# Splitting a product's result straight out of PSUM on ACT and DVE, and one ACT function for product and sigmoid

## The chip, the cores and the metric

The kernel runs on one core of one Trainium2 chip. The engines are PE (matmul), DVE (vector), ACT (scalar functions), POOL (general) and SP (issues DMAs). The metric is the device time of one execution in microseconds (us); the time of a kernel is the median of its runs.

## What is computed

Inputs are f32 or wider; NT = 2304 tokens of width 512. Attention with a pooled and a local part comes first, then a mixture of experts with one expert a token, then a dense two-layer block:

```
x = attention(q, k, v)                              # 2304 x 512
xc = x[x @ w_skip > 0];  e_idx = argmax(xc @ w_gate)
for e in range(8):                                  # w1[e] 512 x 1024, w2[e] 1024 x 512
    h = np.maximum(xc[mask] @ w1[e], 0.0)
    y[mask] = gate_w[mask, None] * (h @ w2[e])
out[do_compute] = xc + y
h = x @ w_in                                        # 512 x 2048
g = h * (1.0 / (1.0 + np.exp(-1.702 * h)))
return g @ w_out                                    # 2048 x 512
```

## The kernel before

Each large product is done in f16 with split operands: a value v becomes a high part (v scaled by a power of two, rounded to f16) and a low part (the scaled value minus the high part, again f16). A product is then three: high x high, high x low, low x high, added in PSUM. So each operand is split on the way, and the name of a tile tells its part: xh and xl, wh and wl, hh and hl, gh and gl.

The program has three stages, `phase_a` (attention and routing, and the split of w_in), `phase_b` (the experts) and `phase_c` (the last block); `overflow` between the last two is a loop that runs only where an expert has more than 192 tokens.

In `phase_b` every expert takes 192 token rows. The steps of an expert are small functions, and a table, `STAGE_B`, gives each a due time in periods of an expert. All steps of all experts are sorted by (expert + due time) and emitted in that order; `in_order` then ties each of PE, ACT, DVE and POOL to this order. So every engine is a queue in a written order, in which steps of three neighbouring experts are mixed. The steps that matter here:

- `load`: SP loads the f32 weights, raw, in four parts of 1 MB; a part's buffer is free again when its wl is made.
- `bound`, `scale`, `scb`: ACT squares and sums the raw weights (jk, L689), PE sums over partitions (psw, L59), DVE makes the scale by some tiny operations (w_e, w_s, w_i, L72 to L78), then iv (L706, L708), the factor that takes the scales back.
- `hi`, `lo`: wh on ACT for one half of a matrix (L715) and on DVE for the other (L717); wl on DVE (L723).
- `gather`, `xprep`, `xh`, `xl`: POOL gathers the token rows by indirect DMA (L768), PE transposes them, ACT and DVE split them.
- `l1`, four parts of two 128-wide columns of the hidden layer: 24 matmuls (L812) into one PSUM tile ph, from a pool of four that also serves psw.
- `l1e`: ACT takes Relu of ph with the factor 2^-20 to an f32 tile ht (L820; two buffers). `l1h`: DVE casts ht to hh (L823). `l1l`: POOL subtracts, hl = ht - hh (L827).
- `l2`, four parts (L839, L846): the second product, from hh, hl and the split w2.
- `giv`, `yrow`, `ymx`, `yadd`, `scatter`: ACT scales the rows of y (L865), DVE takes their maximum (L871), POOL adds them to the token rows (g, L881) and scatters these by indirect DMA (L902). `scat` on POOL writes token numbers (ids, L911).

In one period the written order on DVE is, with the expert in brackets: xl(0), lo00(0), lo10(-1), l1h2(-1), ymx(-2), l1h3(-1), hi11(-1), hi01(0), lo11(-1), lo01(0), l1h1(0), l1h0(0), scb(0), giv(-1). On ACT: l1e2(-1), bound00(1), l1e3(-1), three bounds, l1e0(0), l1e1(0), xh(1), hi00(1), hi10(0), yrow(-1). On PE: xprep(1), l10(0), l11(0), l20 to l22(-1), scale(0), l23(-1), l12(0), l13(0). On POOL: l1l1(-1), scat0(0), l1l2(-1), gather(2), l1l3(-1), yadd0(-2), scatter0(-2), scat2(-1), yadd1(-2), scatter1(-2), scat1(0), l1l0(0).

In `phase_c` the tokens go in six blocks of 384. `l1` of a block has 16 steps of 12 matmuls (L1097) into ph, a PSUM tile from a pool of three; ACT takes the sigmoid with a scale (L1101), DVE multiplies with ph and a factor (sg, L1102), and one step later `late` casts sg to gh on ACT (L1089) and subtracts to gl (L1090), on POOL in the first three blocks and on DVE after that. `l2` of a block (L1117) follows two blocks behind. During the first two and a half blocks `Wout` splits w_out: on ACT w64a (L126), w64j (L231) and woh (L242), on DVE w64l and w64f (L130 to L132) and wol (L243); these steps are put behind the steps of `l1` by `behind`, which holds them to the order in which they are emitted.

Of the kernel before, what the change touches and what calls it, by code (L numbers as in the profile page):

```python
# [18 lines left out]
P = 128  # L19
# [15 lines left out]
CAP = 192  # L35
# [3 lines left out]
XW = 2 * XH  # L39
NB = 384  # L40
NTC = NB // P
C20 = 2.0 ** -20
ONE = float(1 << 23)

# [22 lines left out]
    return ps[:, P:P + 1]  # L67


def pow2_into(nc, e, s, si, m, squared):  # L70
    V = nc.vector
    V.tensor_scalar(e, m.bitcast(I32), 0x7F800000, None, op0=ALU.bitwise_and)  # L72
    if squared:
        V.tensor_scalar(e, e, 0.5, 64.0 * ONE, op0=ALU.mult, op1=ALU.add)
        V.tensor_scalar(e, e, 0x7F800000, None, op0=ALU.bitwise_and)
    V.tensor_scalar(e, e, 64.0 * ONE, 200.0 * ONE, op0=ALU.max, op1=ALU.min)
    V.tensor_scalar(s.bitcast(I32), e, -1.0, 268.0 * ONE, op0=ALU.mult, op1=ALU.add)  # L77
    V.tensor_scalar(si.bitcast(I32), e, 14.0 * ONE, None, op0=ALU.subtract)  # L78


def pow2_scale(nc, pool, m, name, squared=False):


    e = pool.tile([P, 1], I32, name=f"{name}_e")
    s = pool.tile([P, 1], F32, name=f"{name}_s")
    si = pool.tile([P, 1], F32, name=f"{name}_i")
    pow2_into(nc, e, s, si, m, squared)
    return s, si


# [7 lines left out]
    csc=3.1751, chl=5.4280)  # L98

STAGE_B = dict(  # L100
    l10=-2.8750, l1e0=-2.5414, l1h0=-2.1815, l1l0=-2.0258, l20=-1.6661, l11=-2.8473, l1e1=-2.5379, l1h1=-2.2714,
    l1l1=-1.8902, l21=-1.5453, l12=-2.1639, l1e2=-1.9897, l1h2=-1.8716, l1l2=-1.8041, l22=-1.3442, l13=-2.0520,
    l1e3=-1.8744, l1h3=-1.8562, l1l3=-1.7262, l23=-1.2374, scale=-2.2810, scb=-2.1764, bound00=-3.9127,
    hi00=-3.1600, lo00=-2.9149, load00=-2.9138, bound01=-3.5859, hi01=-2.6890, lo01=-2.5881, load01=-2.5870,
    bound10=-2.7781, hi10=-2.1111, lo10=-1.8915, load10=-1.8904, bound11=-2.5563,
    hi11=-1.7296, lo11=-1.6624, load11=-1.6613, gather=-4.7500, xprep=-3.9203, xh=-3.5055, xl=-2.9872,
    giv=-1.1000, yrow0=-1.0047, yrow1=-1.0040, ymx=-0.8644, yadd0=-0.6966, scatter0=-0.6711,
    yadd1=-0.6113, scatter1=-0.6009, scat0=-2.8208, scat1=-2.5500, scat2=-1.6433)


# [554 lines left out]
class Experts:  # L665
# [30 lines left out]
    def scale2(self, i, ix):  # L696
        nc, sm = self.nc, self.sm
        m2 = self.m2.pop(i)
        e = sm.tile([P, 2], I32, tag="w_e", name="w_e")
        s, si = (sm.tile([P, 2], F32, tag=f"w_{n}", name=f"w_{n}", bufs=3) for n in ("s", "i"))  # L700
        pow2_into(nc, e, s, si, m2, True)
        for wi in range(2):
            self.s[i + 1 - wi, wi] = s[:, wi:wi + 1], si[:, wi:wi + 1]
        if i >= 0:
            iv = sm.tile([P, 1], F32, tag="iv", name="iv")
            nc.vector.scalar_tensor_tensor(iv, self.s[i, 0][1], 1.0 / C20, self.s[i, 1][1],  # L706
                                           op0=ALU.mult, op1=ALU.mult)
            nc.vector.tensor_tensor(iv, iv, ix, ALU.mult)  # L708
            self.iv[i] = iv

    def hi(self, e, wi, hf, on_act):
# [15 lines left out]
def phase_b(ctx, tc, c, ex):  # L727
    nc = tc.nc
    ident = c["ident"]
    V, A, G, T = nc.vector, nc.scalar, nc.gpsimd, nc.tensor  # L730
    wk = ctx.enter_context(tc.tile_pool(name="b_wk", bufs=2))
    sm = ctx.enter_context(tc.tile_pool(name="b_sm", bufs=2))
# [23 lines left out]
    V.tensor_reduce(xb, c["xm"], axis=AX.X, op=ALU.max)  # L756
    mp = max_all(nc, c, psh.tile([P, 512], F32, tag="psh", name="psm"), sm.tile([1, 1], F32, name="xb0", bufs=1), xb)
    V.tensor_copy(c["xmax"], mp)
    sx, ix = pow2_scale(nc, c["cp"], c["xmax"], "sx")
    ex.onesf, ex.ps = c["onesf"], lambda: psh.tile([P, 512], F32, tag="psh", name="psw")  # L760

    xg, xs, hts, gv, phs, pxs, pys, hr, yr = {}, {}, {}, {}, {}, {}, {}, {}, {}

    def gather(e):
        g0 = wk.tile([P, XW], F32, tag="g0", name="g0", bufs=5)
# [48 lines left out]
                    n += 1  # L814
        phs[e, fp] = ph

    def l1e(e, fp):
        ph, (hh, hl) = phs.pop((e, fp)), hts[e]
        hr[e, fp] = t = wk.tile([P, 2, CAP], F32, tag="ht", name="ht")
        A.activation(t, ph, AF.Relu, scale=C20)  # L820

    def l1h(e, fp):
        V.tensor_copy(hts[e][0][:, 2 * fp:2 * fp + 2, :], hr[e, fp])  # L823

    def l1l(e, fp):
        hh, hl = hts[e]
        G.tensor_tensor(hl[:, 2 * fp:2 * fp + 2, :], hr.pop((e, fp)), hh[:, 2 * fp:2 * fp + 2, :], ALU.subtract)  # L827

    def l2(e, i):

# [195 lines left out]
def phase_c(ctx, tc, c, win, wih, wil, w_out, out):  # L1026
    nc = tc.nc
    ident = c["ident"]
    V, A, T = nc.vector, nc.scalar, nc.tensor
# [27 lines left out]
    sinv = sm.tile([P, 1], F32, name="sinv")
    V.tensor_reduce(sinv, win.si, axis=AX.X, op=ALU.max)
# [73 lines left out]
    n, m = steps[-1][0] + 2, ahead * (DF // P) + DF // P // 2  # L1132
# [146 lines left out]
```

## Time and profile before

| | us |
|---|---|
| median of 3 runs | 803.38 (798.86 to 803.81) |
| the profiled execution | 801.5, its span 799.7 |
| busy PE / DVE / ACT / POOL | 694.6 / 478.1 / 394.0 / 297.7 |
| mean granted clock of PE | 0.948 of full speed |

The span is the time from the first to the last instruction that the profiler saw; what lies around it is 1.8 us. Busy time is a mean over stages that differ, so a stage is read by itself: the experts run from about 205 to 387 us, the last stage from about 393 us to the end.

### The profile page before, as it was taken

How to read it: one execution, taken by the hardware profiler on the slowest of the kernel's cores; microseconds unless marked ns; L12 is line 12 of the kernel's file. 1: busy time of each engine (PE TensorE's matmuls, PEld its weight loads, DVE VectorE, ACT ScalarE, POOL GpSimd, SP SyncE). 2: the span in 40 equal slices, each digit the busy share in tenths (PEclk: the TensorE clock that was granted, in tenths of full speed). 3: DMA queues.
4: the chain of work that ended last, by engine and by line, in shares of the span. 5: the costliest groups of instructions: out<-in, count | busy, mean ns of one | idle time of the engine just before them, and what ended most of it. 6: DMA issues, size and time to landing. Idle time of an engine off the chain costs nothing.

```text
span 799.7 us, 15485 instructions
## 1 busy us (share of the span) xinstructions
PE 694.6 (87%) x6207; PEld 430.8 (54%) x6207; DVE 478.1 (60%) x909; ACT 394.0 (49%) x806; POOL 297.7 (37%) x294
## 2 busy tenths in 40 slices
PE   4478978878499899878499899999999999999997
PEld 3355655655376666655265555545545545544443
DVE  8889997996588888899468996204503511520000
ACT  1566665763687667763167876414413412421111
POOL 8555644650346999987334444300000000000000
PEclk9977997999599999999799999999999999999999
DMA  9956998617456666520344331001000000000000
GB/s 259 263 152 174 301 285 260 158 33 258 113 205 237 241 234 240 189 73 16 119 132 146 123 102 27 1 26 54 1 27 14 1 13 27 1 14 27 27 27 27
DMA packets 43007, 92.49 MB, mean 116 GB/s; under 512 B 10398, under 2 KB 24354, under 8 KB 38837
## 3 DMA queue, kind: packets, MB, share of 16 engines
q1 hardware_dynamic: 25908, 81.11, 31.6%
q10 hardware_dynamic: 14208, 4.87, 2.6%
q0 software_dynamic: 2816, 5.50, 2.4%
q8 instruction: 50, 0.82, 0.4%
q14 instruction: 25, 0.20, 0.1%
HBM read 79.55 MB, written 12.92 MB: 116 GB/s over the span
## 4 chain that ended last, share of the span: by engine, by line
PE 48%; DVE 19%; POOL 11%; issue 9%; DMA 8%; ACT 4%; SPq 1%; POOLq 0%; ACTq 0%; DVEq 0%
PE po L1117 22%; PE ph L1097 17%; DMA w64r<-in_moe_w_in 5%; POOL hl L827 3%; DVE wl L723 3%; POOL g L881 3%; DVE w64l L131 2%; POOL ids L911 2%; POOL g L768 2%; DVE sg L1102 2%; DVE w64f L132 1%; DVE wol L243 1%; PE po L464 1%; DVE w64l L130 1%; DMA vw<-in_vwin 1%
## 5 line engine op out<-in xcount | busy, mean ns | idle before, releaser
L1102 DVE SCALAR_TENSOR_TENSOR sg<-ph,gs,sg 128x384 f32<-128x384 f32 x96 | 58.7, 615 | 132.3 <-ACT sg L1101 132.1
L1097 PEld LDWEIGHTS <-wih 128*128 128x128 f16 x768 | 76.2, 100 | 60.1 <-issue 12.4
L1123 ACT ACTIVATE o<-po,os 128x128 f32<-128x128 f32 x72 | 20.5, 367 | 148.8 <-PE po L1117 93.4
L1117 PEld LDWEIGHTS <-gh 128*128 128x128 f16 x576 | 56.3, 98 | 66.0
L1097 PE MATMUL ph<-xh,wih 128*128 128x384 f16 x384 | 79.5, 330 | 8.4 <-DVE sg L1102 7.5
L723 DVE SCALAR_TENSOR_TENSOR wl<-raw,w_s,wh 128x2048 f16<-128x2048 f32 x32 | 81.3, 2574 | 4.4 <-ACT wh L715 2.9
L1097 PE MATMUL ph<-xh,wil 128*128 128x384 f16 x384 | 79.9, 330 | 0.0
L1090 POOL TENSOR_TENSOR gl<-sg,gh 128x384 f16<-128x384 f32 x48 | 49.2, 1027 | 81.7 <-ACT gh L1089 63.2
L1097 PE MATMUL ph<-xl,wih 128*128 128x384 f16 x384 | 78.9, 328 | 0.0
L1089 ACT CAST gh<-sg 128x384 f16<-128x384 f32 x96 | 48.8, 509 | 47.8 <-DVE sg L1102 47.6
L1101 ACT ACTIVATE sg<-ph,ih 128x384 f32<-128x384 f32 x96 | 55.4, 578 | 33.2 <-PE ph L1097 31.1
L1117 PE MATMUL po<-woh,gh 128*128 128x512 f16 x288 | 67.1, 379 | 0.0
L689 ACT ACTIVATE jk<-raw 128x2048 f16<-128x2048 f32 x32 | 61.1, 1908 | 9.3 <-DVE mx L686 8.7
L1117 PE MATMUL po<-wol,gh 128*128 128x512 f16 x288 | 65.3, 379 | 0.0
L1117 PE MATMUL po<-woh,gl 128*128 128x512 f16 x288 | 65.1, 379 | 0.0
L827 POOL TENSOR_TENSOR hl<-ht,hh 128x384 f16<-128x384 f32 x32 | 43.5, 1372 | 27.2 <-DVE hh L823 17.4
L1097 PEld LDWEIGHTS <-wil 128*128 128x128 f16 x384 | 38.0, 99 | 25.5 <-issue 1.2
L812 PEld LDWEIGHTS <-wh 128*128 128x128 f16 x512 | 44.1, 101 | 4.4 <-ACT wh L715 2.3
L1117 PEld LDWEIGHTS <-gl 128*128 128x128 f16 x288 | 28.2, 98 | 34.0
L715 ACT ACTIVATE wh<-raw,w_s 128x2048 f16<-128x2048 f32 x16 | 31.3, 1995 | 29.6 <-DVE w_s L77 18.2
L1090 DVE TENSOR_TENSOR gl<-sg,gh 128x384 f16<-128x384 f32 x48 | 26.8, 558 | 26.5 <-ACT gh L1089 26.5
L812 PE MATMUL ph<-xh,wl 128*128 128x192 f16 x256 | 32.7, 252 | 3.9 <-DVE wl L723 3.6
(228 smaller groups left out, 1343.5 us busy)
## 6 DMA issues: line engine op xcount, KB each, us to landing
raw<-in_moe_w SPq DMA_DIRECT2D x32, 1024.0 KB
w64r<-in_moe_w_in SPq DMA_DIRECT2D x16, 512.0 KB
w64r<-in_moe_w_out SPq DMA_DIRECT2D x16, 512.0 KB
vw<-in_vwin SPq DMA_DIRECT2D x32, 216.0 KB
qt<-in_q SPq DMA_DIRECT2D x16, 288.0 KB
kt<-in_k SPq DMA_DIRECT2D x16, 288.0 KB
vn<-in_v SPq DMA_DIRECT2D x16, 288.0 KB
xd<-xn ACTq DMA_DIRECT2D x16, 288.0 KB
```

The costliest lines, as they stand in the source:

```text
L689: self.nc.scalar.activation(j, r, AF.Square, accum_out=self.mx[i][:, hf, wi:wi + 1])
L715: self.nc.scalar.activation(t, r, AF.Copy, scale=s)
L723: self.nc.vector.scalar_tensor_tensor(t, r, s, self.h[e, wi, hf], op0=ALU.mult, op1=ALU.subtract)
L812: T.matmul(ph[:, fi, :], wa[:, k_, o:o + P], xa[:, k_, :], start=(n == 0), stop=(n == 3 * NK - 1))
L827: G.tensor_tensor(hl[:, 2 * fp:2 * fp + 2, :], hr.pop((e, fp)), hh[:, 2 * fp:2 * fp + 2, :], ALU.subtract)
L881: G.tensor_tensor(g, g, yr[e][:, cols(ti)].rearrange("p (h w) -> p h w", w=DM // 2), ALU.add)
L1089: A.copy(split[1], split[0])
L1090: (nc.gpsimd if b <= ahead else V).tensor_tensor(split[2], split[0], split[1], ALU.subtract)
L1097: T.matmul(ph, wa[:, k_, f * P:(f + 1) * P], xx[:, k_, :], start=(n == 0), stop=(n == 3 * NK - 1))
L1101: A.activation(sg, ph, AF.Sigmoid, scale=ih[:, f:f + 1])
L1102: V.scalar_tensor_tensor(sg, ph, gs[:, f:f + 1], sg, op0=ALU.mult, op1=ALU.mult)
L1117: T.matmul(po, ga[:, f, i * P:(i + 1) * P], wa[:, f, :], start=(n == 0), stop=(n == 3 * (DF // P) - 1))
```

## The change

In the experts `l1e` and ht go. ACT writes hh from ph directly, as f16 (`l1h`), at the due times that `l1e` had; DVE makes hl from ph and hh (`l1l`), at the due times that `l1h` had; POOL has no part in it any more. The powers of two move: the scales s get other constants (t, XT, WT), so that ph needs no factor, and iv is one operation and no longer two. In the last stage ACT has one function, Gelu_apprx_sigmoid of the scaled ph, which is the product of its argument with the sigmoid of 1.702 times it; `late` then makes gh on ACT with a scale and gl on DVE in all blocks, from sg and gh.

```
+XT, WT = 3, 8
-def pow2_into(nc, e, s, si, m, squared):
+def pow2_into(nc, e, s, si, m, squared, t=15):
...
-    V.tensor_scalar(s.bitcast(I32), e, -1.0, 268.0 * ONE, op0=ALU.mult, op1=ALU.add)
-    V.tensor_scalar(si.bitcast(I32), e, 14.0 * ONE, None, op0=ALU.subtract)
+    V.tensor_scalar(s.bitcast(I32), e, -1.0, (253.0 + t) * ONE, op0=ALU.mult, op1=ALU.add)
+    V.tensor_scalar(si.bitcast(I32), e, (t - 1.0) * ONE, None, op0=ALU.subtract)
...
-    l10=-2.8750, l1e0=-2.5414, l1h0=-2.1815, l1l0=-2.0258, ...
+    l10=-2.8750, l1h0=-2.5414, l1l0=-2.1815, ...
...
-            nc.vector.scalar_tensor_tensor(iv, self.s[i, 0][1], 1.0 / C20, self.s[i, 1][1],
-                                           op0=ALU.mult, op1=ALU.mult)
-            nc.vector.tensor_tensor(iv, iv, ix, ALU.mult)
+            nc.vector.scalar_tensor_tensor(iv, self.s[i, 0][1], ix, self.s[i, 1][1], op0=ALU.mult, op1=ALU.mult)
...
-    def l1e(e, fp):
-        ph, (hh, hl) = phs.pop((e, fp)), hts[e]
-        hr[e, fp] = t = wk.tile([P, 2, CAP], F32, tag="ht", name="ht")
-        A.activation(t, ph, AF.Relu, scale=C20)
-
     def l1h(e, fp):
-        V.tensor_copy(hts[e][0][:, 2 * fp:2 * fp + 2, :], hr[e, fp])
+        A.activation(hts[e][0][:, 2 * fp:2 * fp + 2, :], phs[e, fp], AF.Relu)

     def l1l(e, fp):
-        hh, hl = hts[e]
-        G.tensor_tensor(hl[:, 2 * fp:2 * fp + 2, :], hr.pop((e, fp)), hh[:, 2 * fp:2 * fp + 2, :], ALU.subtract)
+        hh, hl = (h[:, 2 * fp:2 * fp + 2, :] for h in hts[e])
+        V.scalar_tensor_tensor(hl, phs.pop((e, fp)), 0.0, hh, op0=ALU.max, op1=ALU.subtract)
...
-    V.tensor_scalar(ih, win.si, ix, 1.702, op0=ALU.mult, op1=ALU.mult)
-    gs = sm.tile([P, NF], F32, name="gs")
-    V.tensor_scalar(gs, win.si, smin, C20, op0=ALU.mult, op1=ALU.mult)
+    V.tensor_scalar(ih, win.si, ix, None, op0=ALU.mult)
+    gs = sm.tile([P, 1], F32, name="gs")
+    V.tensor_scalar(gs, sx, smin, C20, op0=ALU.mult, op1=ALU.mult)
...
-                A.copy(split[1], split[0])
-                (nc.gpsimd if b <= ahead else V).tensor_tensor(split[2], split[0], split[1], ALU.subtract)
+                A.activation(split[1], split[0], AF.Copy, scale=gs)
+                V.scalar_tensor_tensor(split[2], split[0], gs, split[1], op0=ALU.mult, op1=ALU.subtract)
...
-            A.activation(sg, ph, AF.Sigmoid, scale=ih[:, f:f + 1])
-            V.scalar_tensor_tensor(sg, ph, gs[:, f:f + 1], sg, op0=ALU.mult, op1=ALU.mult)
+            A.activation(sg, ph, AF.Gelu_apprx_sigmoid, scale=ih[:, f:f + 1])
```

## Rows read from the trace of the kernel before

**Rows 1.** Windows, one expert: length; busy us PE, PEld, DVE, ACT, POOL; clock; DMA; GB/s.

```profile
299.91:320.82 20.91, 18.22 (x180) 13.21 (x180) 18.50 (x23) 15.03 (x18) 19.04 (x13) 1.00 0.67 240
```

**Rows 2.** Timeline, DVE, experts: start, us, engine, line, operation, idle before and releaser.

```profile
223.88 0.15 DVE L72 TENSOR_SCALAR w_e<-psw 128x2 int32<-128x2 int32 x1
...
298.97 5.27 DVE L723 SCALAR_TENSOR_TENSOR wl<-raw,w_s,wh 128x2048 f16<-128x2048 f32 x2
304.16 1.69 DVE L823 CAST hh<-ht 128x384 f16<-128x384 f32 x2
305.77 0.15 DVE L72 TENSOR_SCALAR w_e<-psw 128x2 int32<-128x2 int32 x1
...
309.00 4.62 DVE L723 SCALAR_TENSOR_TENSOR wl<-raw,w_s,wh 128x2048 f16<-128x2048 f32 x2
314.95 0.53 DVE L823 CAST hh<-ht 128x384 f16<-128x384 f32 x1 [1.33 <-ACT ht L820]
...
317.21 0.36 DVE L823 CAST hh<-ht 128x384 f16<-128x384 f32 x1 [0.88 <-ACT ht L820]
317.49 2.48 DVE L717 TENSOR_SCALAR wh<-raw,w_s 128x2048 f16<-128x2048 f32 x2
319.88 2.35 DVE L723 SCALAR_TENSOR_TENSOR wl<-raw,w_s,wh 128x2048 f16<-128x2048 f32 x1
...
367.91 0.15 DVE L72 TENSOR_SCALAR w_e<-psw 128x2 int32<-128x2 int32 x1
```

**Rows 3.** Timeline, ACT, the same expert.

```profile
306.97 3.90 ACT L715 ACTIVATE wh<-raw,w_s 128x2048 f16<-128x2048 f32 x2 [3.19 <-DVE w_s L77]
310.77 1.03 ACT L865 ACTIVATE yr<-py,giv 128x512 f32<-128x512 f32 x2
314.42 0.49 ACT L820 ACTIVATE ht<-ph 128x384 f32<-128x384 f32 x1 [2.62 <-POOL hl L827]
```

**Rows 4.** Timeline, POOL, the same expert.

```profile
302.05 3.31 POOL L881 TENSOR_TENSOR g<-g,yr 128x512 f32<-128x512 f32 x1
...
312.17 3.10 POOL L827 TENSOR_TENSOR hl<-ht,hh 128x384 f16<-128x384 f32 x2
```

**Rows 5.** Lines L723 and L1102, all instances: ns minimum/median/maximum, first and last start.

```profile
L723 DVE SCALAR_TENSOR_TENSOR wl<-raw,w_s,wh x32: 2334/2350/3721, 214.4 to 378.2; 128x2048 f16<-128x2048 f32 x32
...
L1102 DVE SCALAR_TENSOR_TENSOR sg<-ph,gs,sg x96: 601/618/620, 406.4 to 707.1; 128x384 f32<-128x384 f32 x96
```

**Rows 6.** Timeline, PE, the same expert.

```profile
301.37 0.59 PE L839 MATMUL py<-wl,hh 128*128 128x512 f16 x2 [1.86 <-DVE wl L723]
...
303.10 0.61 PE L59 MATMUL psw<-mx,onesf 128*128 128x2 f32 x4
...
319.07 0.60 PE L839 MATMUL py<-wh,hh 128*128 128x512 f16 x2
```

**Rows 7.** Waits of PE, 399 to 492 us: us in total, times, longest.

```profile
PE ph L1097 <- DVE sg L1102: 7.5, 8, 2.2
```

**Rows 8.** Windows of the last stage, columns as in rows 1.

```profile
399.00:492.00 93.00, 84.58 (x519) 52.62 (x519) 75.70 (x129) 69.57 (x146) 37.00 (x35) 0.96 0.35 114
480.00:490.00 10.00, 9.03 (x48) 5.36 (x48) 5.62 (x14) 7.09 (x15) 4.68 (x5) 0.83 0.10 26
```

**Rows 9.** Chain that ended last: start, us, engine, line and count.

```profile
498.32 5.85 PE ph L1097 x36
```

**Rows 10.** Groups on DVE, 399 to 492 us: busy us, mean ns, idle before.

```profile
L132 DVE SCALAR_TENSOR_TENSOR w64f<-w64a,w64l 128x512 int32<-128x512 int32 x16 | 14.8, 923 | 0.2
L243 DVE SCALAR_TENSOR_TENSOR wol<-w64f,wo_s,woh 128x512 f16<-128x512 f32 x14 | 14.3, 1026 | 1.3 <-ACT woh L242 1.3
```

**Rows 11.** Lines L132 and L243, all instances, columns as in rows 5.

```profile
L132 DVE SCALAR_TENSOR_TENSOR w64f<-w64a,w64l x32: 670/683/1291, 12.1 to 479.7; 128x512 int32<-128x512 int32 x32
...
L243 DVE SCALAR_TENSOR_TENSOR wol<-w64f,wo_s,woh x16: 740/752/1404, 436.3 to 498.5; 128x512 f16<-128x512 f32 x16
```

**Rows 12.** Timeline, ACT, start of the last stage.

```profile
399.63 1.28 ACT L1101 ACT_TABLE_LOAD   x1
```

More of the change, by code (lines that the diff above doesn't have):

```diff
@@ L76, in pow2_into, with pow2_scale @@
     V.tensor_scalar(e, e, 64.0 * ONE, 200.0 * ONE, op0=ALU.max, op1=ALU.min)
-    V.tensor_scalar(s.bitcast(I32), e, -1.0, 268.0 * ONE, op0=ALU.mult, op1=ALU.add)
-    V.tensor_scalar(si.bitcast(I32), e, 14.0 * ONE, None, op0=ALU.subtract)
-def pow2_scale(nc, pool, m, name, squared=False):
+    V.tensor_scalar(s.bitcast(I32), e, -1.0, (253.0 + t) * ONE, op0=ALU.mult, op1=ALU.add)
+    V.tensor_scalar(si.bitcast(I32), e, (t - 1.0) * ONE, None, op0=ALU.subtract)
+def pow2_scale(nc, pool, m, name, squared=False, t=15):
     e = pool.tile([P, 1], I32, name=f"{name}_e")
@@ L86, in pow2_scale @@
     si = pool.tile([P, 1], F32, name=f"{name}_i")
-    pow2_into(nc, e, s, si, m, squared)
+    pow2_into(nc, e, s, si, m, squared, t)
     return s, si
@@ L100 @@
 STAGE_B = dict(
[L101 to L107, printed above, removed]
+    l10=-2.8750, l1h0=-2.5414, l1l0=-2.1815, l20=-1.6661, l11=-2.8473, l1h1=-2.5379, l1l1=-2.2714, l21=-1.5453,
+    l12=-2.1639, l1h2=-1.9897, l1l2=-1.8716, l22=-1.3442, l13=-2.0520, l1h3=-1.8744, l1l3=-1.8562, l23=-1.2374,
+    scale=-2.2810, scb=-2.1764, bound00=-3.9127, hi00=-3.1600, lo00=-2.9149, load00=-2.9138, bound01=-3.5859,
+    hi01=-2.6890, lo01=-2.5881, load01=-2.5870, bound10=-2.7781, hi10=-2.1111, lo10=-1.8915, load10=-1.8904,
+    bound11=-2.5563, hi11=-1.7296, lo11=-1.6624, load11=-1.6613, gather=-4.7500, xprep=-3.9203, xh=-3.5055,
+    xl=-2.9872, giv=-1.1000, yrow0=-1.0047, yrow1=-1.0040, ymx=-0.8644, yadd0=-0.6966, scatter0=-0.6711,
     yadd1=-0.6113, scatter1=-0.6009, scat0=-2.8208, scat1=-2.5500, scat2=-1.6433)
@@ L700, in scale2 @@
         s, si = (sm.tile([P, 2], F32, tag=f"w_{n}", name=f"w_{n}", bufs=3) for n in ("s", "i"))
-        pow2_into(nc, e, s, si, m2, True)
+        pow2_into(nc, e, s, si, m2, True, WT)
         for wi in range(2):
@@ L758, in phase_b @@
     V.tensor_copy(c["xmax"], mp)
-    sx, ix = pow2_scale(nc, c["cp"], c["xmax"], "sx")
+    sx, ix = pow2_scale(nc, c["cp"], c["xmax"], "sx", t=XT)
     ex.onesf, ex.ps = c["onesf"], lambda: psh.tile([P, 512], F32, tag="psh", name="psw")
-    xg, xs, hts, gv, phs, pxs, pys, hr, yr = {}, {}, {}, {}, {}, {}, {}, {}, {}
+    xg, xs, hts, gv, phs, pxs, pys, yr = {}, {}, {}, {}, {}, {}, {}, {}
     def gather(e):
@@ L928, in phase_b @@
     for i in range(NK):
-        for fn in (l1, l1e, l1h, l1l, l2):
+        for fn in (l1, l1h, l1l, l2):
             fns[f"{fn.__name__}{i}"] = lambda e, fn=fn, i=i: fn(e, i)
```

## The prediction

> **What bounds the kernel now.** I read the busy time by window first, then the timelines of each engine through one expert, then the waits and the chain in the last stage. The attention stage is not touched. The change sits in two places: the expert stage, from about 205 to 387 us, and the last stage, from about 393 us to the end.
>
> In the expert stage no engine is idle for long: over 20.9 us PE is busy 18.2, DVE 18.5 and POOL 19.0 [rows 1]. So the windows don't name the bound, and the reader has to follow one engine round. DVE does it without a gap except for two [rows 2]: it begins the tiny scale operations (scb) at 223.88 for the first expert and at 367.91 for the eighth, so seven periods take 144.03 us, 20.6 each. In the period from 298.97 the pieces are: two wl 5.19 (to 304.16), two hh casts 1.61 (to 305.77), scales to the next wl 3.23, two wl 4.62, an idle 1.33 that ends with ACT's ht, cast and ymx 1.38, a second idle 0.88, cast 0.28, two wh 2.39: 20.9. That is the whole period, so DVE's queue is the loop, and the two idle pieces belong to it. Why was ACT late? Its ht had itself waited 2.62 us for POOL's hl [rows 3], as the ht buffers are two and hl of the same expert's first pair is the reader that frees one. POOL gave that hl at 312.17, after the row addition (3.31) and its DMA issues [rows 4]. So POOL sets about 2.2 us of each period from outside, and something more by slowing DVE: a wl takes 2.35 us at the median but up to 3.72 [rows 5], and the pair in this period took 5.19 where the other took 4.62.
>
> PE is close behind. It waited 1.86 us for wl at 301.37, then it had 1.73 us left of that l2 part, and from 303.10, where the scale sums begin, to 319.07, where the same l2 part of the next expert begins, it waited for nobody [rows 6]. With that part's first pair of 0.4 to 0.6 its own work per expert is 15.97 + 1.73 + 0.4 = 18.1, a floor that no change of the other engines moves.
>
> In the last stage PE is busy to the end, and its wait for others is small: 7.5 us in eight waits, all for DVE's sg to free a PSUM buffer [rows 7], and all before about 490 us, while DVE also splits w_out. From 399 to 492 us DVE is busy 75.7 of 93 us, ACT 69.6 [rows 8], both in lumps. Behind one of these waits PE's clock falls: the 10 us from 480 have 0.83 granted, a mean of the levels 1.2 and 2.4 GHz, and so up to 1.7 us more are lost.
>
> **The change, expert stage.** ACT: ht (Relu to f32) becomes hh (Relu to f16), one for one, same tile from PSUM; I cost it at nothing, since ACT has nearly 6 us idle a period [rows 1]. DVE: 32 casts leave and 32 subtractions out of PSUM come. The nearest row is sg in the last stage, 128x384 with one operand in PSUM, 601 to 620 ns in 96 instances [rows 5], as long beside POOL as without it; starts would be some 0.55 to 0.6 apart. The casts took 0.28 to 0.45 undisturbed, and 1.61 for a pair beside POOL [rows 2]. So the bill on DVE is between +0.3 and -0.25 each; taken piece by piece below, the four come to about 2.3 where the casts took 2.3 in this period. Here a rule speaks against the change. VectorE: DVE Perf Modes of the Trainium skill (Rules for kernel authors) says of elementwise work on a matmul's output to accept the slow mode out of PSUM, or to copy it to SBUF first where there are many operations; the kernel before is its second way. By that rule against undisturbed casts 32 x 0.3 = some 10 us of DVE would go onto the loop; sg's row agrees on the price out of PSUM, and whether the casts' disturbed length was the usual one no row of before decides.
>
> POOL: 32 hl leave, some 1.5 us each where a pair takes 3.10 [rows 4]. Everything queued behind them on POOL moves earlier: the row addition, the scatters, the gathers, the ids DMAs. Nobody waits for these in the middle of the loop, only at its end. The idle 1.33 and 0.88 go, since ACT's next hh needs no buffer that POOL frees: ACT ends yrow at 311.8 and could run hh 2.6 us before it ran ht [rows 3], ahead of DVE's need at 313.6. The PSUM tiles are freed by DVE now, no longer by ACT. There are four. The first to feel it would be the last pair of an expert's first product, which takes over the first pair's tile. Behind the wl that PE waits for, PE still has the rest of that l2 part (1.73), the scale sums, a whole l2 part and the pair before; at least 1.73 + 2.1 + 1.9 = 5.7 us. DVE has one more wl and two hl, 2.35 + 1.2 = 3.6. So a margin of 2 us covers it, and on ACT, PE and POOL nothing is queued behind the subtraction but through this tile; behind it on DVE stand the scales, by 0.6 us later each.
>
> The new period, by the queue of DVE: two wl 4.6 to 5.2, two hl 1.15, scales 3.2 (they end on ACT's wh, not on DVE), two wl 4.6, hl, ymx and hl 2.0 (1.38 + 0.28, the two casts longer by 0.15 to 0.3), two wh 2.4: 18.0 to 18.6. The dropped multiplication in iv lies under the wait for wh, so nothing. What is late next is PE's 18.1. I take 18.4: (20.6 - 18.4) x 7 = 15.2 us. Bounds: 17.9 if the rows of PE are a little long (18.7 us), and 19.6 if POOL's additions and descriptors collide with the wl as hl did (7 us). Weight loads follow: 240 GB/s over a period at 0.67 of the DMA engines [rows 1] would be 273 GB/s at 0.76, not full. Ramp: the first scb comes 0.5 us later, as two longer operations stand before it. Tail: behind 367.91 DVE has the same queue once more, and the longest wl, 3.72 for 2.35 [rows 5], lies in it: 1.5 us, or nothing if the collisions remain.
>
> **The change, last stage.** DVE's product sg goes; gl on DVE takes its place, in the first three blocks new (POOL had it), later in place of a subtraction. That is about 0.6 for 0.6, so DVE's count there is not smaller. What changes is who waits: the PSUM tile is freed by ACT's one function, DVE is out of the loop of ph, and ACT's gh no longer waits for DVE, so what is queued behind it on ACT, the w_out steps and the next step's function, comes earlier. Second, POOL is empty: the w_out operations w64f and wol have a mean of 0.92 and 1.03 there [rows 10], a median of 0.68 and 0.75 over the whole kernel and 1.29 and 1.40 at most [rows 11], and I take the long ones to be those beside POOL's gl. The excess is 16 x 0.24 + 14 x 0.27 = 7.6 us for these two alone. Without it DVE has at most 68 us of work in the 84 that PE needs (93 less 7.5 and 1.7), and three sg buffers of slack. On ACT a scaled copy stands in for the cast; yrow's pair of scaled copies, 768 columns, takes 1.03 [rows 3], so 384 take 0.5 to 0.6, about the cast. ACT is busy 69.6 of 93 us [rows 8], which covers it; if that cover goes, PE waits for ACT. I count 7.5 + 1.7 - 2.2 left over = 7 us; bounds 1 (ACT takes DVE's place) and 9.2. After 500 us PE has no wait, so the rest of the edit gives nothing there.
>
> **Sum.** 15.2 - 0.5 + 1.5 + 7 = 23.2. The profiled execution took 801.5 (its span is 799.7, and the 1.8 around it stay), so 778.3; it is 0.2% under the median of the runs (803.4), and I say 779.
>
> **Rivals.** (a) POOL's removed work is not the cause of the slow DVE rows; addition and descriptors do it too, and starting earlier they meet other wl. For it: POOL's addition of 3.31 us lay beside the long pair [rows 2, 4]. Against it: hl lay beside that pair too, and is most of what leaves. Period 19.6, tail nothing: 801.5 - 7 + 0.5 - 7 = 788. The same comes out if the casts mostly took their undisturbed length, so that DVE pays 32 x 0.3 on top: 778.3 + 9.6. (b) ACT becomes what ph waits for: it sits behind w64j, which waits for DVE's w64f, and behind sg buffers that gl frees. Against it: ACT is the less busy of the two [rows 8]. Last stage 1 us: 784; with (a) too, 794. (c) Slower: the new function's table doesn't hold Copy and Square. Before, the stage has a single ACT_TABLE_LOAD of 1.28 us [rows 12], though Sigmoid, Copy and Square alternate. If the new set is without them, each of 96 steps has two loads, so ACT needs 0.6 + 0.6 + 2.57 = 3.8 us a step where PE needs 5.85 / 3 = 1.95 [rows 9]: 96 x 1.8 = 173 us, some 950. It decides from the point where a step's loads exceed ACT's spare 0.75 us, so at one load a step already. ScalarE: Activation LUTs (Table sets: the hidden batching unit) of the Trainium skill says that cheap functions such as copy are in every set, and that gelu_apprx_sigmoid isn't in gelu's; by the first half the load stays single. It doesn't name Square. (d) The change doesn't do what it says, as the period is PE's with its coupling to wl: the idle pieces merely move to another wait, and both stages together give under 8 us: 795 to 803.
>
> **Chances.** Forecast 0.62, (a) 0.15, (b) 0.10, (c) 0.03, (d) 0.07, and 0.03 for something slower that I don't see. The range takes in the bounds 18.7 and 9.2 at the low side (801.5 + 0.5 - 18.7 - 1.5 - 9.2 = 772.6, and less if the wl get shorter still) and (a) with (b) at the high: 770 to 794. One per cent, 8 us, is about what a measurement of this kernel can tell from no change; so faster is forecast, (a) and (b), 0.87; same is (d), 0.07; slower is (c) and the unseen, 0.06.
>
> **What would show it.** Right: the scb of first and eighth expert 129 us apart; no idle of DVE before hl or of ACT before hh; sg's wait gone from PE's list; w64f and wol near their medians; a single table load. Wrong: a new wait of PE for DVE's hl (the margin was misread), DVE's wl still long beside POOL, PE waiting for ACT's function, or the period staying at 20 with PE idle inside it.

## The result and the profile after

The changed kernel takes 767.05 us, the median of 4 runs (764.29 to 770.5), where the kernel before took 801.54 in the runs beside it (798.86 to 803.81): a ratio of 0.9573, 95% interval 0.9519 to 0.9627. The forecast was 779 with a range from 770 to 794, so the sign and the places were right, and the gain was half as large again as forecast: 34.5 us against the 23.2 of the sum.

Where it came from is read by stage, from the timelines of the two profiled executions (after: 764.29 us, span 762.6):

| stage | before | after | gain | forecast |
|---|---|---|---|---|
| to the end of the routing | 204.3 | 200.6 | 3.8 | 0 |
| from there to scb of expert 0 | 19.6 | 19.6 | -0.1 | -0.5 |
| seven periods, scb of expert 0 to 7 | 144.0 | 123.6 | 20.4 | 15.2 |
| to the last expert's row addition | 18.4 | 15.9 | 2.5 | 1.5 |
| to the first matmul of the last stage | 13.4 | 12.8 | 0.6 | 0 |
| last stage | 400.0 | 390.1 | 9.9 | 7 |
| span | 799.7 | 762.6 | 37.1 | 23.2 |

The first line is not the change's. The kernels of this study do the same work there, and in their profiles the routing ends anywhere from 200.6 to 213.7 us; a second set of runs of the changed kernel (after_again, below) had it at 208.6. The other lines make 33.3 us.

**Experts.** The timeline of DVE in the changed kernel, answering to [rows 2] (start, us, engine, line, operation, idle before and releaser):

```profile
220.19 0.15 DVE L73 TENSOR_SCALAR w_e<-psw 128x2 int32<-128x2 int32 x1
...
272.39 0.16 DVE L73 TENSOR_SCALAR w_e<-psw 128x2 int32<-128x2 int32 x1
...
275.64 4.61 DVE L721 SCALAR_TENSOR_TENSOR wl<-raw,w_s,wh 128x2048 f16<-128x2048 f32 x2 [0.72 <-ACT wh L713]
280.17 0.55 DVE L820 SCALAR_TENSOR_TENSOR hl<-ph,hh 128x384 f16<-128x384 f32 x1
280.64 0.94 DVE L864 TENSOR_REDUCE ym<-yr 128x1 f32<-128x768 f32 x1
281.50 0.54 DVE L820 SCALAR_TENSOR_TENSOR hl<-ph,hh 128x384 f16<-128x384 f32 x1
281.96 2.72 DVE L715 TENSOR_SCALAR wh<-raw,w_s 128x2048 f16<-128x2048 f32 x2
284.60 4.60 DVE L721 SCALAR_TENSOR_TENSOR wl<-raw,w_s,wh 128x2048 f16<-128x2048 f32 x2
289.13 1.01 DVE L820 SCALAR_TENSOR_TENSOR hl<-ph,hh 128x384 f16<-128x384 f32 x2
290.28 0.16 DVE L73 TENSOR_SCALAR w_e<-psw 128x2 int32<-128x2 int32 x1
...
343.81 0.14 DVE L73 TENSOR_SCALAR w_e<-psw 128x2 int32<-128x2 int32 x1
```

The first and the last row are 123.62 us apart, 17.7 a period; from 272.39 to 290.28 it is 17.89. No hl waits in the loop, and both pairs of wl take 4.6 here; in four of the seven periods the second pair takes 5.08, and these are no longer (17.7 to 18.0). Windows of the changed kernel, columns as in [rows 1]: one period, then the last stage in three pieces, which answer to [rows 8].

```profile
273.64:291.53 17.89, 17.89 (x183) 13.28 (x184) 16.89 (x21) 14.90 (x18) 13.51 (x9) 1.00 0.78 271
...
372.49:382.49 10.00, 10.00 (x49) 5.75 (x49) 1.88 (x3) 4.09 (x7) 0.00 (x0) 0.71 0.28 97
382.49:465.00 82.51, 82.51 (x534) 52.59 (x532) 67.89 (x139) 76.33 (x152) 0.00 (x0) 1.00 0.36 119
465.00:762.60 297.60, 293.27 (x1530) 149.75 (x1527) 37.98 (x61) 88.40 (x187) 0.00 (x0) 1.00 0.05 19
```

In the period PE is busy without a break, 17.89 of 17.89, where before it was 18.22 of 20.91; the list of its waits from 226 to 344 us is empty. So PE's own work now fills the period, and DVE, with 16.89 of work and 0.72 of waiting for ACT's wh, stands close behind. POOL has fallen from 19.0 to 13.5.

**Last stage.** PE is busy for the whole of the first 92.5 us, and its only wait is the one at the start of the stage; the 7.5 us of [rows 7] are gone. Waits of PE (us in total, times, longest), the chain (start, us, line, count; answers to [rows 9]), groups on DVE from 372 to 465 us (answer to [rows 10]) and the instances of ACT's new function (answer to [rows 12]), all of the changed kernel:

```profile
PE ph L1090 <- ACT xh L1069: 0.8, 1, 0.8
```

```profile
452.18 23.40 PE ph L1090 x144
```

```profile
L243 DVE SCALAR_TENSOR_TENSOR wol<-w64f,wo_s,woh 128x512 f16<-128x512 f32 x16 | 12.0, 747 | 0.0
...
L132 DVE SCALAR_TENSOR_TENSOR w64f<-w64a,w64l 128x512 int32<-128x512 int32 x16 | 11.0, 686 | 0.1
```

```profile
L1094 ACT ACTIVATE sg<-ph,ih x96: 555/580/592, 379.6 to 665.1; 128x384 f32<-128x384 f32 x96
...
L1094 ACT ACT_TABLE_LOAD  x1: 1283/1283/1283, 372.5 to 372.5; - x1
```

The granted clock is 1.00, the upper of its two levels (2.4 GHz), from 382.49 on; the fall to 0.83 behind a wait [rows 8] does not occur. 144 matmuls in 23.40 are 0.1625 each, as the 36 in 5.85 were: PE works no faster, it only no longer stops. w64f and wol have fallen from 923 and 1026 ns to 686 and 747, within 5 ns of the medians of [rows 11]. The new function takes 580 ns and its table is loaded once, so rival (c) is out.

### The profile page after: what moved, and what is told of

Same layout as the page of the kernel before. It is cut to its first block, busy times and chain, and to the rows that moved or that the text cites. A ratio compares the mean times of both kernels' runs of the same rounds, so it can differ in the third digit from the quotient of the medians.

```text
span 762.6 us, 15293 instructions
## 1 busy us (share of the span) xinstructions
PE 686.8 (90%) x6207; PEld 427.8 (56%) x6207; DVE 421.9 (55%) x853; ACT 403.1 (53%) x806; POOL 221.2 (29%) x214
## 4 chain that ended last, share of the span: by engine, by line
PE 65%; DMA 10%; DVE 8%; issue 7%; ACT 5%; POOL 4%; SPq 1%; POOLq 0%; ACTq 0%; DVEq 0%
PE ph L1090 25%; PE po L1109 23%; PE ph L810 5%; DMA w64r<-in_moe_w_in 4%; PE py L832 3%; DMA xd<-xn 3%; POOL ids L904 2%; ACT sd L383 2%; PE py L839 2%; PE lg L530 1%; PE px L1067 1%; DMA vw<-in_vwin 1%; DMA xd<-g,idu 1%; POOL g L874 1%; DVE wil L192 1%
## 5 line engine op out<-in xcount | busy, mean ns | idle before, releaser
L1083 DVE SCALAR_TENSOR_TENSOR gl<-sg,gs,gh 128x384 f16<-128x384 f32 x96 | 59.1, 617 | 181.9 <-ACT gh L1082 181.6
L721 DVE SCALAR_TENSOR_TENSOR wl<-raw,w_s,wh 128x2048 f16<-128x2048 f32 x32 | 75.8, 2406 | 7.2 <-ACT wh L713 6.4
L1109 PE MATMUL po<-woh,gh 128*128 128x512 f16 x288 | 65.1, 379 | 0.0
L1082 ACT ACTIVATE gh<-sg,gs 128x384 f16<-128x384 f32 x96 | 58.8, 613 | 2.5
L874 POOL TENSOR_TENSOR g<-g,yr 128x512 f32<-128x512 f32 (+1 forms) x14 | 30.6, 2183 | 23.9 <-ACT yr L858 23.7
L126 ACT ACTIVATE w64a<-w64r 128x512 f32<-128x512 f32 x32 | 21.4, 668 | 27.1 <-DMA w64r<-in_moe_w_in 26.7
L810 PE MATMUL ph<-xh,wh 128*128 128x192 f16 x256 | 33.1, 254 | 1.8 <-ACT wh L713 1.8
L904 POOL DMA_INDIRECT ids<-tok,slt x24 | 32.2, 1343 | 7.3 <-issue 6.7
```

Of the source, the lines that this page charges most:

```text
L721: self.nc.vector.scalar_tensor_tensor(t, r, s, self.h[e, wi, hf], op0=ALU.mult, op1=ALU.subtract)
L810: T.matmul(ph[:, fi, :], wa[:, k_, o:o + P], xa[:, k_, :], start=(n == 0), stop=(n == 3 * NK - 1))
L874: G.tensor_tensor(g, g, yr[e][:, cols(ti)].rearrange("p (h w) -> p h w", w=DM // 2), ALU.add)
L904: d = G.indirect_dma_start(c["ids"], IOA(ap=c["slt"][:TB, j:j + 1], axis=0), c["tok"][:TB, j:j + 1], None, bounds_check=RMAX - 1, oob_is_e ...
L1082: A.activation(split[1], split[0], AF.Copy, scale=gs)
L1083: V.scalar_tensor_tensor(split[2], split[0], gs, split[1], op0=ALU.mult, op1=ALU.subtract)
```

## The experiments

The theory at this point was that of the prediction: DVE lost time in the experts by waiting for ACT's ht, which waited for POOL's hl, and some more by operations that POOL slowed; in the last stage, that sg stood behind slow w_out operations on DVE. The rivals: that collisions of DVE with POOL are all of it; that PE's own work is the bound and the rest follows; that in the last stage only one of the two halves matters. Four kernels were compared first with the kernel before (805.15, 19 runs), then four more (beside 805.68, 7 runs), then three (beside 803.81, 7 runs).

### One half at a time

experts_only is the changed kernel with the last stage of before; last_only is the kernel before with the last stage of the change. The core of the first, against the change (the second has it the other way round, against before):

```
-            A.activation(sg, ph, AF.Gelu_apprx_sigmoid, scale=ih[:, f:f + 1])
+            A.activation(sg, ph, AF.Sigmoid, scale=ih[:, f:f + 1])
+            V.scalar_tensor_tensor(sg, ph, gs[:, f:f + 1], sg, op0=ALU.mult, op1=ALU.mult)
...
-                A.activation(split[1], split[0], AF.Copy, scale=gs)
-                V.scalar_tensor_tensor(split[2], split[0], gs, split[1], op0=ALU.mult, op1=ALU.subtract)
+                A.copy(split[1], split[0])
+                (nc.gpsimd if b <= ahead else V).tensor_tensor(split[2], split[0], split[1], ALU.subtract)
```

> The change in the experts alone; the last stage is that of before. Theory: the two stages are independent, and the experts gave 20.4 us in the seven periods and 2.5 in the tail, so about 801.5 - 23 = 778.5, with a period of 17.7 and PE's 7.5 us of waits for DVE's sg still there in the last stage. Rival: part of the gain seen in the last stage came from the experts (loads of w_out or PE's clock); then this run gives more than 26 us.

> The change in the last stage alone; the experts are those of before. Theory: 801.5 - 10.5 = 791, period of the experts 20.6 as before, no wait of PE in the last stage but the one for xh. Rival: the part of the last stage was mis-read from two single profiles and gives the 7 us that I counted, 794.5.

experts_only: 786.86 us (783.64 to 789.92), 0.9775 [0.9717, 0.9833]; last_only: 793.92 (790.93 to 798.79), 0.9872 [0.9808, 0.9936]. The two together make 18.3 + 11.2 = 29.5 us, near the whole change's 30.9 in after_again and below the first runs' 34.5. By stage they separate cleanly: seven periods 123.8 and last stage 400.6 in the first, 143.4 and 389.0 in the second. The halves are independent. The times themselves lie above the expected 778.5 and 791, by 8 and 3 us; the stages are as expected, and in these two profiles the routing ended 6 and 3 us later than in that of before. PE's waits in the last stage of experts_only are those of [rows 7]:

```profile
PE ph L1090 <- DVE sg L1095: 7.5, 8, 2.2
```

### Taking the wait alone away

ht4 is the kernel before with four ht buffers, so that ACT's ht no longer waits for POOL:

```
-        hr[e, fp] = t = wk.tile([P, 2, CAP], F32, tag="ht", name="ht")
+        hr[e, fp] = t = wk.tile([P, 2, CAP], F32, tag="ht", name="ht", bufs=4)
```

> Before, with four ht buffers for two, so that ACT need not wait for POOL's hl; POOL keeps hl and its place beside DVE. Theory 1 (the waits are the loss): DVE's idle 1.33 and 0.88 go, period 20.6 to 18.4, tail as before, 801.5 - 15 = 786. Theory 2 (POOL slows DVE, and the waits are only where the slack shows): the period stays at 20 or more, 797 to 802. Theory 3 (POOL's own queue, 19.0 us of work a period, is the bound behind the waits): period 19.0 to 19.5, 801.5 - 9 = 792, with PE or ACT waiting for POOL somewhere else.

805.34 us, ratio 1.0006 [0.9976, 1.0037]: nothing. Seven periods take 142.9 us. The period stays at 20.4, the second theory's outcome. All casts of the kernel before (ns minimum/median/maximum), then the timelines of DVE and POOL in ht4:

```profile
L823 DVE CAST hh<-ht x32: 346/360/1420, 223.3 to 376.5; 128x384 f16<-128x384 f32 x32
```

```profile
302.65 2.40 DVE L823 CAST hh<-ht 128x384 f16<-128x384 f32 x2
...
313.85 1.78 DVE L823 CAST hh<-ht 128x384 f16<-128x384 f32 x1
315.56 3.43 DVE L717 TENSOR_SCALAR wh<-raw,w_s 128x2048 f16<-128x2048 f32 x2
```

```profile
301.31 2.18 POOL L827 TENSOR_TENSOR hl<-ht,hh 128x384 f16<-128x384 f32 x1
303.45 1.37 POOL L881 TENSOR_TENSOR g<-g,yr 128x512 f32<-128x512 f32 x1
...
313.62 1.79 POOL L827 TENSOR_TENSOR hl<-ht,hh 128x384 f16<-128x384 f32 x2
```

The idle pieces in front of the casts are gone, and the casts themselves have become as long: 2.40 for a pair and 1.78 for one, against a median of 0.36 in the kernel before. Over the seven periods DVE's idle pieces shrink by 9.2 us, and casts and wh grow by 12.8. Each of the two ends 0.2 us after the operation of POOL that runs beside it (at 305.05 and 304.82; at 315.63 and 315.41). The wait was only where the time showed. Behind it stood DVE being held up while POOL reads and writes SBUF. So the reading of the two idle pieces as POOL's price "from outside" fell.

### Taking hl off POOL, but staying in SBUF

hl_dve_sbuf is ht4 with hl on DVE, right behind its cast. POOL carries the same steps as in the change, and DVE has a cast beside each subtraction; the operands of both are in SBUF:

```
-        G.tensor_tensor(hl[:, 2 * fp:2 * fp + 2, :], hr.pop((e, fp)), hh[:, 2 * fp:2 * fp + 2, :], ALU.subtract)
+        V.tensor_tensor(hl[:, 2 * fp:2 * fp + 2, :], hr.pop((e, fp)), hh[:, 2 * fp:2 * fp + 2, :], ALU.subtract)
```

> Before, with hl on DVE out of ht and hh in SBUF and four ht buffers; POOL has no part in it, DVE has a cast and a subtraction for each pair. Theory: DVE's queue grows by four times (0.28 + 0.47 - 0.48) = 1.1 us against the changed kernel, so its period is 18.6 to 19.0 and PE waits for DVE; 801.5 - 13 = 788. Rival (the rule that a copy to SBUF pays where a result is read twice): as short as the changed kernel, period 17.7, 779.

807.83 us, 1.0071 [1.0025, 1.0116]; seven periods 144.6 us: neither the 788 of the theory nor the 779 of the rival. DVE's and POOL's timelines:

```profile
305.20 0.35 DVE L823 CAST hh<-ht 128x384 f16<-128x384 f32 x1
305.65 0.56 DVE L827 TENSOR_TENSOR hl<-ht,hh 128x384 f16<-128x384 f32 x1
...
314.57 1.43 DVE L823 CAST hh<-ht 128x384 f16<-128x384 f32 x1
...
317.82 1.06 DVE L827 TENSOR_TENSOR hl<-ht,hh 128x384 f16<-128x384 f32 x1
318.80 2.94 DVE L717 TENSOR_SCALAR wh<-raw,w_s 128x2048 f16<-128x2048 f32 x2
```

```profile
312.56 3.23 POOL L881 TENSOR_TENSOR g<-g,yr 128x512 f32<-128x512 f32 x1 [3.93 <-ACT yr L865]
```

Undisturbed, cast and subtraction are some 0.9 us from start to start (305.20 to 306.13, where the next cast starts), so two blocks cost 1.8 where two hl out of PSUM cost 1.0: four of them are 1.6 us more a period. The rest of the 3.0 us between this period (20.7 in the mean) and the change's 17.7 is held-up operations, now beside POOL's row additions and DMA issues: a cast of 1.43, a subtraction of 1.06, a wh pair of 2.94. VectorE: DVE Perf Modes of the Trainium skill (Rules for kernel authors) has it that a matmul's output may be copied to SBUF first where many operations follow. How many are many it doesn't say; for the two here the copy is the slower way: with two readers, both out of PSUM, the period is 17.7 us, and with the copy 20.7.

### Putting POOL's work back

pool_ballast is the changed kernel in which POOL does an operation of hl's shape at hl's old due times. It reads zeros and hh and writes a tile that nobody reads, so no engine waits for it:

```
+    def l1x(e, fp):
+        t = wk.tile([P, 2, CAP], F16, tag="hx", name="hx")
+        G.tensor_tensor(t, c["zero"][:, 0:2 * CAP].rearrange("p (a b) -> p a b", a=2),
+                        hts[e][0][:, 2 * fp:2 * fp + 2, :], ALU.subtract)
```

> The changed kernel with POOL doing a subtraction of hl's size again, at hl's old due times, reading hh and a constant and writing a tile that nobody reads: hl's work on POOL without anybody waiting for it. Theory 1 (only the waits were lost): POOL's work is beside the loop, period 17.7 to 17.9, 767 to 769. Theory 2 (POOL's reads slow DVE's operations with two inputs in SBUF): wl and wh grow by 1 to 1.5 us a period, of which DVE's 0.7 us of slack hides a half; period 18.4, 772, and means of wl of 2.5 us or more. Theory 3 (POOL's queue): 18.5 us or more, yrow waiting for POOL's addition.

792.47 us, 0.9844 [0.9796, 0.9891]; seven periods 140.3 us, so 16.7 of the 20.4 are lost again, and neither PE nor ACT nor DVE waits for POOL once. The sign is the second theory's, the size is not: a mean period of 20.0 where it had 18.4. DVE's timeline and groups (225 to 345 us: busy us, mean ns, idle before), and POOL's timeline:

```profile
307.81 6.00 DVE L721 SCALAR_TENSOR_TENSOR wl<-raw,w_s,wh 128x2048 f16<-128x2048 f32 x2 [0.68 <-ACT wh L713]
...
317.91 6.78 DVE L721 SCALAR_TENSOR_TENSOR wl<-raw,w_s,wh 128x2048 f16<-128x2048 f32 x2
```

```profile
L721 DVE SCALAR_TENSOR_TENSOR wl<-raw,w_s,wh 128x2048 f16<-128x2048 f32 x24 | 69.7, 2944 | 4.3 <-ACT wh L713 4.3
...
L820 DVE SCALAR_TENSOR_TENSOR hl<-ph,hh 128x384 f16<-128x384 f32 x24 | 12.6, 546 | 0.0
```

```profile
307.59 1.80 POOL L824 TENSOR_TENSOR hx<-zero,hh 128x384 f16<-128x384 f32 x2
...
318.13 0.92 POOL L824 TENSOR_TENSOR hx<-zero,hh 128x384 f16<-128x384 f32 x1
319.01 1.26 POOL L879 TENSOR_TENSOR g<-g,yr 128x512 f32<-128x512 f32 x1
```

The pair of wl that begins at 317.91 takes 6.78, 2.2 more than the 4.60 of the changed kernel; the two operations of POOL beside it take 0.92 + 1.26 = 2.2. wl, with two operands in SBUF, is held up by about what POOL works beside it. hl, with one operand in PSUM, stays at 546 ns. Over the seven periods wl takes 13.1 us more than in the change, most of the 16.7.

ballast_memset tells reading from writing: POOL's extra operation only writes (917 ns, as hx).

```
+        t = wk.tile([P, 5, CAP], F32, tag="hx", name="hx")
+        G.memset(t, 0.0)
```

> As the run with ballast on POOL, but the ballast is a memset of 960 f32 a partition, which reads nothing. Theory (it is POOL's reading of SBUF that holds up DVE's operations with two inputs there): wl falls back to about 2.4 us, period 17.7 to 18.2, 3 us at most over the changed kernel. Rival (POOL's time in its queue, or any use of SBUF by POOL, sets the period): wl stays near 2.9 and the period at 20.

786.33 us (782.18 to 796.27), 0.9753 [0.9675, 0.9832]; seven periods 137.4 us. wl falls back as the theory had it, but its period, 17.7 to 18.2, was missed. DVE's and POOL's timelines:

```profile
243.13 0.16 DVE L73 TENSOR_SCALAR w_e<-psw 128x2 int32<-128x2 int32 x1 [1.14 <-PE psw L60]
...
261.02 0.16 DVE L73 TENSOR_SCALAR w_e<-psw 128x2 int32<-128x2 int32 x1
...
301.50 2.45 DVE L77 TENSOR_SCALAR w_e<-w_e 128x2 int32<-128x2 int32 x1
...
306.23 4.61 DVE L721 SCALAR_TENSOR_TENSOR wl<-raw,w_s,wh 128x2048 f16<-128x2048 f32 x2 [0.68 <-ACT wh L713]
```

```profile
302.17 1.75 POOL L824 MEMSET hx<- 128x960 f32 x2
```

wl is as in the changed kernel (4.61), so it takes POOL's reading to hold up wl. But one tiny scale operation, two columns wide and 0.17 us in the changed kernel, now takes 2.45: it ends at 303.95, when the two memsets end at 303.92. It stands on the way from the scales to ACT's wh and from there to wl, and the steady period (19.95) is 2.06 longer than 17.89. Six of the seven periods have such an operation, of 2.41 to 2.45; the one that has none, from 243.13 to 261.02, takes 17.89, as in the change. So there are two kinds: two-operand work (wl) is held up by POOL's reads, and a single-operand tensor_scalar by its writes too. For the cast this split isn't shown: the operations of POOL beside the long casts read and write.

This agrees with SBUF — State Buffer of the Trainium skill (Who interferes with whom): an instruction of DVE with two inputs in SBUF contends with one of GpSimd (POOL here) that reads SBUF, not with one that only writes; copies, casts and tensor_scalar can enter modes in which one of the two engines blocks for a whole instruction; one with at most one SBUF input, outside those modes, doesn't contend. The rows here go with each of the three: wl at 2944 and 2446 ns beside reading and writing ballast, w_e at 2.45 us, hl at 546 ns. In which mode w_e ran no trace says.

### Lightening DVE, with hl on POOL

hl_pool_act2 is the changed kernel with hl on POOL from an f32 ht that ACT writes beside hh (four buffers); DVE then has neither cast nor hl, 2.0 us a period less than in the change.

```
+        hr[e, fp] = t = wk.tile([P, 2, CAP], F32, tag="ht", name="ht", bufs=4)
+        A.activation(t, phs.pop((e, fp)), AF.Relu)
...
-        V.scalar_tensor_tensor(hl, phs.pop((e, fp)), 0.0, hh, op0=ALU.max, op1=ALU.subtract)
+        G.tensor_tensor(hl, hr.pop((e, fp)), hh, ALU.subtract)
```

> The changed kernel with hl back on POOL, from an f32 ht that ACT takes out of PSUM beside hh (four ht buffers): DVE has neither cast nor subtraction, 1.9 us a period less than in the changed kernel, nobody waits for POOL but l2, and ACT has 1.9 us more. Theory (collisions with POOL's reads are what cost the period): wl's pairs at 6 us and more as with the ballast, period 18.5 to 19.5 in spite of DVE's shorter list, 775 to 782. Rival (DVE's count of operations sets the period): PE's 17.7 to 17.9, as the changed kernel.

788.66 us, 0.9802 [0.9736, 0.9869]; seven periods 138.6 us, 15 more than in the change although DVE's list is shorter. DVE's and POOL's timelines:

```profile
302.90 2.67 DVE L75 TENSOR_SCALAR w_e<-w_e 128x2 int32<-128x2 int32 x1
...
314.03 4.11 DVE L715 TENSOR_SCALAR wh<-raw,w_s 128x2048 f16<-128x2048 f32 x2
318.06 5.55 DVE L721 SCALAR_TENSOR_TENSOR wl<-raw,w_s,wh 128x2048 f16<-128x2048 f32 x2
```

```profile
303.41 0.92 POOL L824 TENSOR_TENSOR hl<-ht,hh 128x384 f16<-128x384 f32 x1
304.27 1.26 POOL L878 TENSOR_TENSOR g<-g,yr 128x512 f32<-128x512 f32 x1
...
314.06 1.79 POOL L824 TENSOR_TENSOR hl<-ht,hh 128x384 f16<-128x384 f32 x2
```

w_e ends at 305.57, POOL's addition beside it at 305.53. The wh pair has 4.11 where the change has 2.47 to 2.73, beside 1.79 us of hl. Over the seven periods wl, wh and the scale operations take 23.9 us more than in the change, and the 15.3 of hl are gone. A smaller part is a wait that the expectation didn't have, of DVE for PE's scale sums (230 to 367 us):

```profile
DVE w_e L73 <- PE psw L60: 3.6, 7, 1.5
```

The theory was right in kind and too small: a mean period of 19.8 for 18.5 to 19.5. The count of DVE's operations isn't what decided; what POOL does beside them decided most of it.

### How far PE is the bound after the change

pe_light is the changed kernel with 24 matmuls an expert fewer in the first product, some 2.0 us of PE's 17.9:

```
-                for k_ in range(NK):
+                for k_ in range(NK if wa is wh else 1):
```

> The changed kernel with three of four matmuls of wl x xh left out in the experts' first product: 24 matmuls, 2.0 us of PE less for an expert. Theory (PE's own work of 17.9 us is the period now): the period falls, down to what DVE's queue and its wait for ACT's wh allow, 17.2 to 17.5, so 3 to 5 us in all. Rival (DVE's queue is the period and PE only keeps up): no change, 17.7 to 17.9.

769.92 us, 0.9547 [0.9499, 0.9596]; seven periods 122.7 us against 123.6. The 14 us of PE's work that left in seven periods gave 0.9, where the theory had 3 to 5 and the rival none; the other kernels with the changed experts and nothing else in them have 123.1 to 123.8. PE waits for wl again (226 to 344 us):

```profile
PE py L832 <- DVE wl L721: 8.2, 6, 1.7
PE ph L810 <- DVE wl L721: 2.4, 2, 1.6
```

So after the change the two are nearly level, and the rival was closer than the theory: PE's work takes 17.89, and with less of it DVE's queue takes 17.7 (the six periods after the first, which is shorter, at 16.43).

### The two halves of the last stage

sg_gl_dve takes POOL out and keeps the sigmoid with DVE's product; gelu_gl_pool has the one function and leaves gl on POOL in the first three blocks, where it leaves out the factor gs. Their cores:

```
+            A.activation(sg, ph, AF.Sigmoid, scale=ih[:, f:f + 1])
+            V.scalar_tensor_tensor(sg, ph, gs[:, f:f + 1], sg, op0=ALU.mult, op1=ALU.mult)
...
+                V.tensor_tensor(split[2], split[0], split[1], ALU.subtract)
```

```
+                if b <= ahead:
+                    nc.gpsimd.tensor_tensor(split[2], split[0], split[1], ALU.subtract)
```

> The changed experts; the last stage as before (sigmoid, product on DVE out of PSUM), but gl on DVE in all blocks, so POOL is out. Theory 1 (the loop through DVE made PE wait): DVE has 0.56 us more a step and still frees ph, PE's waits stay at 7 us or grow; 777 to 782. Theory 2 (POOL's gl slowed DVE, and that made it late): w64f and wol fall to their medians, 8 to 13 us of DVE go against 36 x 0.56 = 20 added; if contention were all, waits of PE would shrink under 4 us and the time be 770 to 773.

> The changed kernel with gl on POOL in the first three blocks (there gl leaves out the factor gs). Theory 1 (the loop through DVE): PE still doesn't wait, 767, though DVE's w64f and wol are long again. Theory 2 (contention): DVE's w_out operations are long, ACT's w64j waits for w64f, the function behind it is late, and PE waits 3 us or more: 770 to 773.

sg_gl_dve: 775.19 us, 0.9639 [0.9575, 0.9704]; gelu_gl_pool: 774.52, 0.9591 [0.9534, 0.9648]. Last stage: 400.0 us with neither, 391.4 with POOL out, 390.0 with the one function, 390.1 with both. PE's waits in sg_gl_dve, then groups on DVE in gelu_gl_pool (382 to 480 us):

```profile
PE ph L1090 <- DVE sg L1095: 0.7, 1, 0.7
```

```profile
L132 DVE SCALAR_TENSOR_TENSOR w64f<-w64a,w64l 128x512 int32<-128x512 int32 x16 | 15.9, 992 | 0.4
L243 DVE SCALAR_TENSOR_TENSOR wol<-w64f,wo_s,woh 128x512 f16<-128x512 f32 x16 | 14.0, 875 | 8.3 <-ACT woh L242 8.3
```

Either half removes nearly all. With DVE in the loop of ph, its slow operations beside POOL reach PE; with DVE out of it, w64f may take 992 ns again and PE waits for nothing of DVE's. The loss needed both.

### The change once more

> The changed kernel once more, on the chip of these runs: seven periods within 1 us of 123.6 and the last stage within 1 us of 390.1, while the attention stage, which no edit touches, ends anywhere between 200 and 214 us.

772.88 us (772.11 to 773.65), 0.9611 [0.9555, 0.9668]; seven periods 123.3, last stage 389.9 us. These are the first runs' stages to 0.4 us; the routing ended 8 us later.

## Why the prediction came out as it did

**The sign and the mechanism of the last stage: right.** sg's wait is gone, w64f and wol are near their medians, the table is loaded once, DVE and ACT keep up. The term was too small: "7.5 + 1.7 - 2.2 left over = 7" measured 9.9. Nothing was left over: idle time of PE fell by 7.8 and its busy time by 2.1 (387.9 to 385.8, by windows over the whole stage), where the forecast had 1.7 as clock. That last part was not split further. Rival (b), ACT in DVE's place, did not come: ACT is busy 76.3 of 82.5 us from 382.49 on and PE waits for none of it.

**The experts' period: right in direction, and the step that failed is its size**, "I take 18.4: (20.6 - 18.4) x 7 = 15.2", which measured 20.4. It went wrong in three places. PE's floor was put at 18.1, from pieces of a trace in which PE had waits; it is 17.89. The list of DVE's pieces kept the range 4.6 to 5.2 for a wl pair and 0.55 to 0.6 for an hl; the first pair took 4.6 and the second 4.6 or 5.1, four hl took 2.0 and not 2.3, and DVE came out just below PE's floor. And a mean of seven periods was set against a steady one: the first period was short in both kernels (19.02 before, 16.49 after), the other six went from 20.84 to 17.86. That is 2.5 + 6 x 2.98 = 20.4. The bound given, 18.7, left out the same first period. The low side of the range was added up to 772.6; by the stages it is 801.5 - 33.3 = 768.2. The 4.4 between them are 1.7 of this period, 1.0 of the tail, 0.7 of the last stage, 0.4 of the ramp and 0.6 before the last stage, for which nothing was counted. The tail gained 2.5 for the 1.5 forecast: its longest wl went from 3.72 to 2.35 as said, but the other wl went from 2.88 to 2.35 and giv from 1.29 to 0.22 as well. The ramp lost 0.1 for 0.5.

**The reason given for that period: half wrong.** The two idle pieces of DVE were taken for POOL's price, "about 2.2 us of each period from outside", and slower DVE operations for an extra. ht4 shows the opposite order: without the wait the same time stands in casts and wh. The gain comes from POOL's hl no longer running beside DVE, and from the cast, which POOL could hold up, giving way to an operation out of PSUM, which it doesn't. Both are needed: hl_dve_sbuf has only the first and pool_ballast only the second. That the direction came out right is in part luck: the waits that the sum took away were worth nothing by themselves, and the change took away with them what stood behind. (312.17 is also not when POOL gave that hl: [rows 4] have the pair beginning there, and ACT's ht begins at 314.42.)

**The rule that spoke against the change** (10 us by undisturbed casts) did not come true, and neither did rival (a): the row addition and descriptors collide a little (a wl pair of 5.08 at 266.38), under PE's cover. The forecast did not ask who pays: POOL's additions are the long ones now, 2.03 us at the median where pool_ballast has 1.26, and only POOL's own scatter waits for them. In hl_dve_sbuf, beside a cast, the same addition does cost DVE time. Rival (d) was wrong as a rival and right as a limit: PE fills the period now, and pe_light shows DVE's queue 0.2 us behind it.

**What stays open**: why the routing ends at times 13 us apart in kernels that do the same there. It adds to the spread of every comparison, and it is part of the distance between 34.5 and the 33.3 of the stages.

## What to carry to other kernels

A wait inside a full queue can be the place where lost time shows and not its cause: give the buffer and look whether the period moves before paying for anything else. When DVE and POOL work side by side, look at the spread of one operation's durations; those that vary may be held up by POOL, as here, and a form of them that reads PSUM may cost more alone and less in company. When a stage's engine becomes the floor, count its work from an unbroken stretch, and forecast the first period by itself.

## What was not expected of the hardware

- An operation of DVE two columns wide, 0.17 us alone, took 2.45 us beside a DMA issue and two memsets of POOL and ended 0.03 us after these; because other engines wait for it, its lateness cost the period 2.06 us. In the changed kernel, where DMA issues of POOL lie beside such operations, none took over 0.43.
- The subtraction out of PSUM, 128x384, took 541 to 558 ns in all 32 instances of the changed kernel and 546 in the mean beside POOL's extra work; casts of the same shape in SBUF took 0.34 to 1.79 in ht4.
- ACT's Gelu_apprx_sigmoid took 580 ns at 128x384 at the median, and scaled copies beside it needed no other table load: one of 1.28 us for the stage.
